# Moving three q turns of a TensorE-bound attention and MLP kernel: one behind the first x tile, one back onto TensorE, one behind the loads of batch 2

## The chip, the cores and the metric

The kernel runs on one core of one Trainium2 chip. Times are device microseconds (us) of one execution of the whole program. A profile shows a span that is about 1.8 us shorter than the measured time: the profiled execution of the kernel before measured 294.14 us and its span is 292.4 us.

Names: PE is TensorE (PEld its weight loads), ACT ScalarE, DVE VectorE, POOL GpSimd and SP SyncE. A *turn* is a transpose: it brings a [128 rows x 512] piece of q or x into the layout that a matmul needs. It is done either on PE (four 128x128 transposes through PSUM, then a copy by ACT or DVE) or by a DMA that transposes on its way ("DMA_TRANSPOSE", issued by SP).

## The reference

```python
def _attn_ref(q, k, v, g_norm):              # q, k, v: [8 batches, 8 heads, 576, 64] f32
    kv = np.einsum('bhsd,bhse->bhde', k, v)  # no softmax: one 64x64 matrix per head
    out = np.einsum('bhsd,bhde->bhse', q, kv)
    rms = np.sqrt(np.mean(out * out, axis=-1, keepdims=True) + 1e-06)
    return out / rms * g_norm

def _moe_ref(x, g_ln, w_ch1, w_ch2):         # x: [8, 576, 512], w_ch1: [512, 2048], w_ch2: [2048, 512]
    mu = np.mean(x, axis=-1, keepdims=True)
    var = np.mean((x - mu) ** 2, axis=-1, keepdims=True)
    xn = (x - mu) / np.sqrt(var + 1e-06) * g_ln
    return x + np.maximum(xn @ w_ch1, 0.0) @ w_ch2
```

The attention output of a batch, its heads side by side, is the x of the MLP. The matmuls take bf16; loads by GpSimd's queue cast on the way.

## The kernel before

The 8 x 576 rows are cut into 36 *tiles* of 128 rows, nine for each pair of batches. A batch gives four whole tiles (*slots* 0 to 3) and 64 rows that are left. The leftovers of two batches share one tile, so each batch has a *fifth slot* with 64 rows of its own and 64 of zeros. For batches 0 and 1 that shared tile is tile 8; batch 2 starts with tile 9.

The program is not written in the order in which it runs. It lists steps, each with an engine, a cost, a sorting key and what it depends on. A small planner in Python simulates the engines and sorts the steps, and they are issued in that order. Moving one step can therefore move others, on any engine.

The q of batch 0 is loaded slot by slot; slots 0 to 3 turn on PE and the fifth by DMA:

```python
for t in (1, 2, 3):
    add_q_turn_pe(0, t, load["q", 0, t], (-4.5, pos[2] - 9, pos[3] - 9)[t - 1],
                  ("ACT", "ACT", "DVE")[t - 1])
...
add_q_turn_dma(0, 4, 5, load["q", 0, 4] + [z1[0]], pos[8] - 41)
adone[0]["qfree"] = adone[0]["qT", 4][0]
```

The q of batch 1 arrives as one load (`qb`). ACT permutes it slot by slot into `qp`; slots 0 and 1 turn on PE, slots 2 and 3 in one DMA, and the fifth in another DMA behind it:

```python
if t < 2:
    add_q_turn_pe(1, t, [qperm, z1[1]], key + 1, ("DVE", "ACT")[t % 2])
elif t > 2:
    add_q_turn_dma(1, *((2, 4) if t == 3 else (4, 5)), [qperm, z1[1]], key + 1)
```

Batch 2's fifth slot of q is loaded into the buffer of batch 0's, so that load waits for batch 0's fifth-slot turn (`qfree`). When all of batch 2's q has landed, ACT permutes it in two pieces, and one DMA turns all five slots; PE then multiplies tile 9's outputs.

GpSimd issues the loads in a fixed order:

```python
pool_load(("q", 0, 1), load_slot(qp[0], q, 0, 1), rate1)
load_w(0, 1)                                   # w_ch1 in four quarters of 512 columns
pool_load(("q", 0, 2), load_slot(qp[0], q, 0, 2), rate1)
load_w(1, 1)
pool_load(("q", 0, 3), load_slot(qp[0], q, 0, 3), rate1)
load_w(2, 1)
load_w(3, 1)
... # zeroing of buffers, then load_w_kv1:
load_w(0, 2)
pool_load(("k", 1), load_kv(kb, k, 1), rate6)
pool_load(("v", 1), load_kv(vb, v, 1), rate6)
load_w(1, 2)
pool_load(("q", 1), load_q(1, 0, 4), rate4, [])
load_w(2, 2)
load_w(3, 2)
```

The first eight tiles run in small pieces (128 rows at a time); from tile 8 on, PE runs *blocks* of 512 rows. The first block matmul, at about 84 us, is used below as a milestone.

Of the kernel before, what the change touches and what calls it, by code (L numbers as in the profile page):

```python
# [14 lines left out]
def kernel(  # L15
# [35 lines left out]
    BANKS = {"mm": 4, "out": 2, "kvt": 2}  # L51
    WARM_FROM = 1.3
    HALVED = (0,)
    SPLIT_STORE = (25,)
    HALF_TURN = (0, 1)
    PARTS = ((0, 4), (4, 8))

# [39 lines left out]
    def add(eng, occ, dur, key, deps, fn, dma=None, alloc=None, main=False, lag=0.0):  # L97
        s = Step()
        s.eng, s.occ, s.dur, s.key, s.fn = eng, occ, dur, key, fn
        s.deps = [d for d in deps if d is not None]  # L100
        s.dma, s.alloc, s.main, s.frees, s.behind = dma, alloc, main, None, None
        s.start = s.done = None
        s.lag = lag
        steps.append(s)
        return s
# [85 lines left out]

    def add_dma(eng, key, deps, fn, nbytes, rate, occ=None, lat=None, tail=None):
        if eng == "POOL":
            s = add(eng, occ or 0.67, 0, key, deps, fn, dma=(1.0, nbytes / rate / 1e3, 0.6))
        else:
            s = add(eng, occ or 0.55, 0, key, deps, fn,
                    dma=(0.6 if lat is None else lat, nbytes / rate / 1e3,
                         0.75 if tail is None else tail))
        return s
# [85 lines left out]
    pos, okey = {}, {}  # L285
    last_pos = {}
    for i, (k_, n, c) in enumerate(groups):
        if k_ == "m1f":
            pos.setdefault(n, i)
            okey.setdefault(n, pos[n] - 20)  # L290
        elif k_ == "m1" and c == 0:
            for j in range(4):
                pos[4 * n + j] = i
                okey[4 * n + j] = i + {2: (-24, 4), 3: (-38, 6)}.get(n, (-44, 8))[0] + j * {2: 4, 3: 6}.get(n, 8)
        elif k_ == "m2":
            last_pos[n] = i

# [9 lines left out]
    load = {}  # L307
# [11 lines left out]
    for eng, f, dst in (("ACT", slice(0, Dm), "gl"), ("DVE", slice(Dm, Dm + D), "gn")):  # L319
        s = add("PE", *((1.8, 2.0) if dst == "gl" else (0.4, 0.6)), -98, row + [ones_done], lambda f=f: spread(f), alloc="mm")  # L320
# [97 lines left out]
    def add_q_turn_pe(b, t, deps, key, eng, h0=0, h1=H):  # L418
        w = (h1 - h0) / H
        s = add("PE", 0.24 * w, 0.24 * w + 0.26, key, [ident] + list(deps), lag=2.0 if t == 4 else 0.0, fn=  # L420
                lambda: q_turn_pe(b, t, h0, h1), alloc=("mm", "kvt")[b])
        occ, dur = act_cost(512 * w) if eng == "ACT" else dve_cost(512 * w, 1.92)
        e = add(eng, occ, dur, key, [s],
                lambda: q_turn_out(b, t, h0, h1, nc.scalar if eng == "ACT" else nc.vector))
        s.frees = e
        adone[b].setdefault(("qT", t), []).append(e)

    def q_turn_dma(b, t0=0, t1=5):
        if "qT" not in att[b]:
# [2 lines left out]
            att[b]["qT"][:, 4 * t0:4 * t1, :],  # L432
            qp[b % 2][:, t0:t1, :, :].rearrange("p t h d -> p (t h d)"))

    def add_q_turn_dma(b, t0, t1, deps, key):
        s = add_dma("SP", key, deps, lambda: q_turn_dma(b, t0, t1), 520.0 * (t1 - t0), 1.0,
                    occ=0.6 * (t1 - t0) + 0.1, lat=0.25, tail=0.42)
        for t in range(t0, t1):
            adone[b].setdefault(("qT", t), []).append(s)

    def kv_mm(b, hps):
        ps = psum.tile([128, HP, 128], f32, tag="kvt", name="kv_ps", bufs=BANKS["kvt"])
# [212 lines left out]
    for h0, h1 in PARTS:  # L655
        add_q_turn_pe(0, 0, load["q", 0, 0, h0], -57 + h0 / 4, ("DVE", "ACT")[h0 // 4], h0, h1)
    for t in (1, 2, 3):
        add_q_turn_pe(0, t, load["q", 0, t], (-4.5, pos[2] - 9, pos[3] - 9)[t - 1],
                      ("ACT", "ACT", "DVE")[t - 1])
    kvs = []  # L660

    urgent = []
    for i, (h0, h1) in enumerate(((0, 4), (4, 6), (6, 8))):
        hps = range(h0 // 2, h1 // 2)
        w = (h1 - h0) / 8
        s = add("PE", 1.36 * w, 1.36 * w + 0.25, -60 + i, load["v", 0, h0] + [k0p[h0 // 4]],
                lambda hps=hps, i=i: kv_mm(0, hps), alloc="kvt")
# [16 lines left out]
    load_w_kv1()  # L684
    pool_load(("q", 0, 4), load_fifth(qp[0][:, 4, :, :], q, 0), 180.0, [])
    pool_load(("q", 1, 4), load_fifth(qp[1][:, 4, :, :], q, 1), 180.0, [])
    add_q_turn_dma(0, 4, 5, load["q", 0, 4] + [z1[0]], pos[8] - 41)
    adone[0]["qfree"] = adone[0]["qT", 4][0]


# [1 line left out]
    def plan_batch(b):  # L692
# [3 lines left out]
        if b == 1:  # L696
            for h0, h1 in ((0, 4), (4, 8)):
                kperm.append(add("ACT", 1.2, 1.35, p - 18, load["k", 1],
                                 lambda h0=h0, h1=h1: k_permute(nc.scalar, 1, h0, h1)))
            for t in range(5):  # L700
                key = (p - 17 + 3 * t) if t < 4 else pos[8] - 40
                if t < 4:
                    qperm = add("ACT", *act_cost(512), key, load["q", 1],
                                lambda t=t: q_permute(nc.scalar, 1, t, t + 1))
                    qread = qperm
                else:
                    qperm = load["q", 1, 4][0]
                if t < 2:
                    add_q_turn_pe(1, t, [qperm, z1[1]], key + 1, ("DVE", "ACT")[t % 2])
                elif t > 2:  # L710
                    add_q_turn_dma(1, *((2, 4) if t == 3 else (4, 5)), [qperm, z1[1]], key + 1)
            vdeps = load["v", 1]
            adone[1]["qread"] = qread
            adone[1]["qfree"] = adone[1]["qT", 4][0]
        else:
            f = FIRST[b]
            def gate(n):

                if b >= 3:
                    m, i = divmod(n, 4)  # L720
                    pool_do(0.1, lambda: nc.gpsimd.tensor_copy(  # L721
                        mark, blk[m]["xT"][:, 0, i * 128:i * 128 + 1]), done[n]["xT"])
            def gate_turn():
                if b >= 3:
                    pool_do(0.1, lambda: nc.gpsimd.tensor_copy(
                        mark, att[b - 1]["qT"][:, 0, 0:1]), [adone[b - 1]["qfree"]])
            dk = [adone[b - 2]["kvmm"]]
            if b < 4:

                pool_do(0.5, lambda: nc.gpsimd.memset(kp[b % 2][no_fifth(b), 4, :, :], 0.0), dk)  # L730
            gate(f - 8 if b > 3 else 5)
            gate_turn()
            by_slot = b >= 3
            if by_slot:
                pool_load(("k", b), load_slots(kp[b % 2], k, b), rate1, dk)
            else:
                pool_load(("k", b), load_kv(kb, k, b), rate4, dk)
            pool_load(("k", b), load_fifth(kp[b % 2][:, 4, :, :], k, b), 180.0, dk)
            def some_q():
                gate(f - 7 if b > 3 else 6)  # L740
                if by_slot:
                    pool_load(("q", b), load_slots(qp[b % 2], q, b), rate1, [adone[b - 2]["qfree"]])
                else:
                    pool_load(("q", b), load_q(b, 0, 4), rate4, [adone[b - 1]["qread"]])
                pool_load(("q", b), load_fifth(qp[b % 2][:, 4, :, :], q, b), 180.0,
                          [adone[b - 2]["qfree"]])
            def some_v():
                gate(f - 6 if b > 3 else 7)
                pool_load(("v", b), load_kv(vb, v, b), rate4, dk)
                pool_load(("v", b), load_fifth(v5[b % 2], v, b), 100.0, dk)  # L750
            for load_some in (some_v, some_q) if b == 2 else (some_q, some_v):
                load_some()
            for h0, h1 in ((0, 4), (4, 8))[by_slot * 2:]:
                kperm.append(add("ACT", 0.85, 1.0, ok - 16, load["k", b][0:1] + dk,
                                 lambda h0=h0, h1=h1: k_permute(nc.scalar, b, h0, h1)))
            qperm = []
            for t0, t1 in ((0, 2), (2, 4))[by_slot * 2:]:
                qperm.append(add("ACT", 0.85, 1.0, ok - 14, load["q", b][0:1] + [
                    adone[b - 2]["qfree"]], lambda t0=t0, t1=t1: q_permute(nc.scalar, b, t0, t1)))
            for x in kperm + qperm:  # L760
                x.lag = 4.0 if b == 2 else 6.0
            kperm += load["k", b]
            turn = add_dma("SP", ok - 12, qperm + load["q", b] + (
                adone[b - 3].get("outs", []) if b >= 3 else []),
                           lambda: q_turn_dma(b), 2.6e3, 1.0, occ=2.98, lat=0.25, tail=0.42)
            for t in range(5):
                adone[b]["qT", t] = [turn]
            adone[b]["qfree"] = turn
            turn.lag = 5.0 if by_slot else 0.0
            adone[b]["qread"] = qperm[-1] if qperm else None  # L770
            vdeps = load["v", b]
# [12 lines left out]
    def plan_tile(n):  # L784
# [4 lines left out]
        deps = []  # L789
# [39 lines left out]
        for h0, h1 in ((0, 4), (4, 8)) if n in HALF_TURN else halves:  # L829
# [12 lines left out]
            else:  # L842
                turned.append(add_dma("SP", q0 + 9, [xc, m1_before], lambda: t_turn_dma(n),
                              0.5e3, 1.0, occ=1.235, lat=0.25, tail=0.42))
        dn["xT"] = turned
        var = [mean]
        if few:
            var.append(add("ACT", 0.68, 0.83, p + 5, xs + dn["xT"], lambda: t_s2(n)))
# [85 lines left out]
    for i, (kind, a, c) in enumerate(groups):  # L934
# [4 lines left out]
                need_tile(4 * a + j)  # L939
        plan_group(i, kind, a, c)  # L940


    def idle_mm(count):
        if "idle" not in blk[0]:
# [50 lines left out]
```

## Time and profile before

| | |
|---|---|
| measured | 294.01 us median of 3 (293.92 to 295.03) |
| span in the profile | 292.4 us |
| PE busy | 284.2 us, 97% |
| next busiest: DVE, ACT | 164.4 us, 143.4 us |
| PE idle ahead of matmuls | 4.74 us in all: 4.07 before 21 us, 0.07 at 39.06, 0.61 at 69.03 |

From the page of the kernel before: busy time, share of the span and instructions of each engine; then the granted clock in 40 slices of the span (9 is full).

```profile
PE 284.2 (97%) x2049; PEld 161.3 (55%) x2049; DVE 164.4 (56%) x357; ACT 143.4 (49%) x292; POOL 65.9 (23%) x93
...
PEclk9999999999999999999999999999999999999999
```

PE is the bottleneck, at full clock. A change of this kind can win only what PE idles, and must pay for all that it adds to PE. The idle time is found in PE's timeline: start in us, duration, line, operation, tile, shape, count, and in brackets the idle time before the group and what ended it. Four stretches of it, before:

```profile
15.55 0.29 PE L550 MATMUL xT_ps<-identity,xc 128*128 128x128 bf16 x2 [0.64 <-DVE xc L543]
16.18 0.40 PE L410 MATMUL qT_ps<-identity,qp 128*128 128x128 bf16 x4 [0.34 <-DMA qp<-in_q_dram]
16.41 0.28 PE L550 MATMUL xT_ps<-identity,xc 128*128 128x128 bf16 x2
...
17.15 0.94 PE L600 MATMUL mm_ps<-xT,w 128*128 128x128 bf16 x14 [0.35 <-ACT xT L557]
17.93 0.39 PE L469 MATMUL out_ps<-kv_pack,qT 128*128 128x128 bf16 x4
18.99 1.07 PE L600 MATMUL mm_ps<-xT,w 128*128 128x128 bf16 x16 [0.68 <-DMA w<-in_moe_w_ch_dram]
...
39.06 0.40 PE L410 MATMUL qT_ps<-identity,qp 128*128 128x128 bf16 x4
...
68.04 0.39 PE L550 MATMUL xT_ps<-identity,xc 128*128 128x128 bf16 x4
69.03 0.62 PE L469 MATMUL out_ps<-kv_pack,qT 128*128 128x128 bf16 x8 [0.61 <-DMA qT<-qp]
```

At 16.18 PE stands 0.34 us for the load of q slot 2, between the two halves of the turn of tile 0's x (L550). Then it stands 0.35 us at 17.15 because x came late, and 0.68 us at 18.99 for the second quarter of w_ch1. At 69.03 it stands 0.61 us for batch 2's q turn. The chain of waits (start, duration, what), followed back from the end, passes through the loads and that turn:

```profile
19.23 19.13 DMA qb<-in_q_dram
...
38.38 0.63 ACT qp L390
...
39.06 0.40 PE qT_ps L410 x4
...
62.45 6.54 DMA qT<-qp
...
69.03 0.62 PE out_ps L469 x8
```

Read it from below: the outputs at 69.03 waited for a turn issued at 62.45; and the PE turn at 39.06 (batch 1, slot 0) waited for ACT, which waited for batch 1's q to land at 38.36. The step at 39.06 shows 0.07 us of idle time.

The DMA turns in SP's queue (the issue of each, with SP's own time for it):

```profile
40.59 5.96 SPq L431 DMA_TRANSPOSE qT<-qp  x3
48.71 3.15 SPq L647 DMA_DIRECT2D out_dram<-x  x4
62.45 3.12 SPq L431 DMA_TRANSPOSE qT<-qp  x1
```

The three turns from 40.59 on are slots 2 and 3 of batch 1, then batch 0's fifth slot (issued at 43.92, landed at 51.78) and last batch 1's fifth slot (issued at 45.31, landed at 53.62). Among the waits (engine, tile, line, released by: us in total, times, longest) is GpSimd's for batch 0's fifth slot, before it may issue batch 2's fifth-slot load:

```profile
POOL qp L256 <- DMA qT<-qp: 10.0, 1, 10.0
```

### The profile page before, as it was taken

To read this page: it belongs to the slowest core of one execution; us is meant where nothing else is said; L and a number is where in the kernel's file an instruction comes from. 1 tells how busy PE (TensorE), PEld (TensorE's weight loads), DVE (VectorE), ACT (ScalarE), POOL (GpSimd) and SP (SyncE) were. 2 spreads that over 40 slices of the span, in tenths; PEclk is the share of its full clock that TensorE was granted. 3 is DMA by queue.
4 is the path that set the end of the run, shared out by engine and by line. 5 is a ranking of instruction groups with operands and counts; after the bars stand their busy time and mean duration, and the time that the engine had idled before them with its cause. 6 is when DMAs were issued, how large, how long until landed. Compare 5 with 4: busy or idle time off the path is not lost.

```text
span 292.4 us, 5167 instructions
## 1 busy us (share of the span) xinstructions
PE 284.2 (97%) x2049; PEld 161.3 (55%) x2049; DVE 164.4 (56%) x357; ACT 143.4 (49%) x292; POOL 65.9 (23%) x93
## 2 busy tenths in 40 slices
PE   8869999999999999999999999999999999999995
PEld 6759945976745445444544445444544444444444
DVE  1597048468883997557655775477557755320022
ACT  3469954887846612761276127611761177017400
POOL 8983320105506405404050406000000000000000
PEclk9999999999999999999999999999999999999999
DMA  7999999943998997993999399932101310120012
GB/s 96 186 199 205 204 198 178 252 73 70 173 171 136 158 183 161 174 203 77 188 103 161 98 181 119 168 81 91 56 18 54 92 54 18 57 86 22 0 74 72
DMA packets 109116, 35.73 MB, mean 122 GB/s; under 512 B 87715, under 2 KB 104739, under 8 KB 109092
## 3 DMA queue, kind: packets, MB, share of 16 engines
q0 software_dynamic: 72624, 18.35, 64.8%
q1 hardware_dynamic: 36228, 16.92, 25.2%
q8 instruction: 16, 0.26, 0.4%
q10 hardware_dynamic: 240, 0.13, 0.2%
q14 instruction: 8, 0.07, 0.1%
HBM read 36.70 MB, written 9.44 MB: 158 GB/s over the span
## 4 chain that ended last, share of the span: by engine, by line
PE 83%; DMA 9%; POOL 6%; issue 0%; ACT 0%; DVE 0%; POOLq 0%
PE mm_ps L634 41%; PE mm_ps L615 33%; DMA qb<-in_q_dram 7%; PE mm_ps L600 4%; PE out_ps L469 3%; PE kv_ps L446 2%; DMA qT<-qp 2%; POOL qp L262 1%; POOL w L342 1%; POOL vb L241 1%; POOL kb L241 1%; PE xT_ps L550 1%; POOL w L344 0%; ACT qp L390 0%; PE qT_ps L410 0%
## 5 line engine op out<-in xcount | busy, mean ns | idle before, releaser
L634 PE MATMUL mm_ps<-w,m 128*128 128x512 bf16 (+2 forms) x608 | 129.5, 368 | 0.0
L615 PE MATMUL mm_ps<-xT,w 128*128 128x512 bf16 x448 | 100.6, 379 | 0.0
L622 ACT ACTIVATE m<-mm_ps 128x512 bf16<-128x512 f32 x112 | 66.8, 597 | 50.3 <-PE mm_ps L615 49.4
L634 PEld LDWEIGHTS <-m 128*128 128x128 bf16 x608 | 57.2, 98 | 60.8
L615 PEld LDWEIGHTS <-w 128*128 128x128 bf16 x448 | 43.1, 98 | 48.8
L491 DVE TENSOR_REDUCE ss<-sq 128x8 f32<-128x512 f32 (+1 forms) x37 | 24.8, 669 | 49.3 <-ACT sq L482 49.3
L641 DVE SCALAR_TENSOR_TENSOR x<-mm_ps,rstd,x 128x512 f32<-128x512 f32 (+2 forms) x38 | 27.3, 720 | 41.8 <-PE mm_ps L634 41.7
L482 ACT ACTIVATE sq<-out_ps 128x512 f32<-128x512 f32 (+1 forms) x37 | 21.6, 583 | 38.4 <-PE out_ps L469 38.3
L600 PE MATMUL mm_ps<-xT,w 128*128 128x128 bf16 x512 | 31.0, 219 | 1.2 <-DMA w<-in_moe_w_ch_dram 0.7
L600 PEld LDWEIGHTS <-w 128*128 128x128 bf16 x512 | 29.3, 98 | 2.5 <-issue 0.9
L543 DVE SCALAR_TENSOR_TENSOR xc<-x,mv,gl 128x512 bf16<-128x512 f32 (+1 forms) x38 | 27.2, 724 | 1.2
L486 DVE TENSOR_TENSOR xg<-out_ps,gn 128x512 f32<-128x512 f32 (+1 forms) x37 | 24.7, 668 | 0.2
L607 ACT ACTIVATE m<-mm_ps 128x512 bf16<-128x512 f32 x32 | 18.5, 597 | 3.2 <-PE mm_ps L600 2.9
L721 POOL COPY mark<-xT 128x1 bf16<-128x1 bf16 x15 | 6.3, 422 | 54.5 <-DMA xT<-xc 52.1
L495 ACT ACTIVATE rms<-ss,eps_attn 128x8 f32<-128x8 f32 (+1 forms) x37 | 11.1, 299 | 12.3 <-DVE ss L491 12.2
L521 DVE TENSOR_TENSOR x<-xg,inv 128x512 f32<-128x512 f32 x24 | 16.6, 691 | 0.8
L537 DVE BATCH_NORM_STATS2 stats<-x 128x6 f32<-128x512 f32 x24 | 16.6, 690 | 0.5
L469 PE MATMUL out_ps<-kv_pack,qT 128*128 128x128 bf16 x160 | 14.5, 219 | 1.3 <-ACT qT L390 0.7
L469 PEld LDWEIGHTS <-qT 128*128 128x128 bf16 x160 | 11.3, 98 | 8.1 <-ACT qT L390 1.1
L446 PEld LDWEIGHTS <-kp 128*128 128x128 bf16 (+1 forms) x168 | 10.6, 101 | 1.9 <-issue 0.3
L446 PE MATMUL kv_ps<-vb,kp 128*128 128x128 bf16 (+1 forms) x144 | 11.3, 226 | 0.2
L557 ACT COPY xT<-xT_ps 128x512 bf16<-128x512 bf16 (+1 forms) x14 | 7.3, 522 | 8.1 <-PE xT_ps L550 8.1
(63 smaller groups left out, 175.2 us busy)
## 6 DMA issues: line engine op xcount, KB each, us to landing
out_dram<-x SPq DMA_DIRECT2D x31, 256.0 KB, 2.3
w<-in_moe_w_ch_dram POOLq DMA_DIRECT2D x8, 512.0 KB, 12.0
vb<-in_v_dram POOLq DMA_DIRECT2D x6, 512.0 KB, 10.9
kp<-in_k_dram POOLq DMA_DIRECT2D x5, 512.0 KB, 8.5
qp<-in_q_dram POOLq DMA_DIRECT2D x5, 512.0 KB, 9.6
qb<-in_q_dram POOLq DMA_DIRECT2D x2, 512.0 KB, 19.1
out_dram<-x SPq DMA_DIRECT2D x8, 128.0 KB, 2.7
qp<-in_q_dram POOLq DMA_DIRECT2D x10, 64.0 KB, 8.7
```

The source lines that it names most:

```text
L446: nc.tensor.matmul(ps[:, hp, :], lhsT=kp[b % 2][p, t, 2 * hp:2 * hp + 2, :].rearrange("p h d -> p (h d)"), rhs=(v5[b % 2][:, 2 * hp:2 * hp ...
L469: nc.tensor.matmul(o3[:, hp, :], lhsT=att[b]["qT"][:, 4 * t + hp, :], rhs=kv_pack[b % 3][:, hp, :], start=(i == 0), stop=(i == len(bs) - 1))
L482: nc.scalar.activation(sq[:, h0:h1, :], st[n]["ps", h0][:, h0:h1, :], func=AF.Square)
L486: nc.vector.tensor_mul(xg[:, h0:h1, :], st[n]["ps", h0][:, h0:h1, :], gn.to_broadcast([128, h1 - h0, D]))
L491: nc.vector.tensor_reduce(ss[:, h0:h1, :], st[n]["sq"][:, h0:h1, :], axis=AX.X, op=ALU.add)
L543: nc.vector.scalar_tensor_tensor(xc[:, f0:f1], in0=st[n]["x"][:, f0:f1], scalar=blk[m]["mv"][:, i, 0:1], in1=gl[:, f0:f1], op0=ALU.subtrac ...
L600: nc.tensor.matmul(ps[:, d, :], lhsT=w1[c][:, kk, d * 128:(d + 1) * 128], rhs=blk[m]["xT"][:, kk, i * 128:(i + 1) * 128], start=(kk == 0), ...
L607: nc.scalar.activation(st[n]["m1"][:, c, :, :], st[n]["m1ps", c], func=AF.Relu)
L615: nc.tensor.matmul(ps, lhsT=w1[c][:, kk, d * 128:(d + 1) * 128], rhs=blk[m]["xT"][:, kk, :], start=(kk == 0), stop=(kk == nKm - 1))
L622: nc.scalar.activation(blk[m]["m1", c][:, d, :], blk[m]["m1ps", g], func=AF.Relu)
L634: nc.tensor.matmul(st[n]["m2ps", f0], lhsT=m1_piece(n, c, d), rhs=w2[c][:, d, f0:f1], start=(c == 0 and d == 0), stop=(c == 3 and d == 3))
L641: nc.vector.scalar_tensor_tensor(x[:, f0:f1], in0=st[n]["m2ps", f0], scalar=blk[m]["rstd"][:, i, :], in1=x[:, f0:f1], op0=ALU.mult, op1=AL ...
```

## The change

It has two parts. **Part A** puts the turn of q slot 2 of batch 0 behind both half turns of tile 0's x, so that x no longer waits for the load of slot 2 at 16.18. **Part B** takes the turn of batch 0's fifth slot back from DMA to PE, and moves the DMA turn of batch 1's fifth slot from about 45 us to about 53 us, behind the loads of batch 2. The aim is to let those loads land earlier and to remove the 0.61 us wait at 69 us. Two smaller edits (a second store split in two near the end; a planner constant that yields three more warm-up matmuls) come along.

```diff
-    SPLIT_STORE = (25,)
+    SPLIT_STORE = (23, 25)
@@ planner's model of a GpSimd load
-            s = add(eng, occ or 0.67, 0, key, deps, fn, dma=(1.0, nbytes / rate / 1e3, 0.6))
+            s = add(eng, occ or 0.67, 0, key, deps, fn, dma=(1.0, nbytes / rate / 1e3, 0.9))
@@ part A
-        add_q_turn_pe(0, t, load["q", 0, t], (-4.5, pos[2] - 9, pos[3] - 9)[t - 1],
-                      ("ACT", "ACT", "DVE")[t - 1])
+        q_turned = add_q_turn_pe(0, t, load["q", 0, t], (-4.5, pos[1] - 3.7, pos[3] - 9)[t - 1],
+                                 ("ACT", "ACT", "DVE")[t - 1])
+        if t == 2:
+            behind_first = q_turned
...
+        if n in HALVED:                      # tile 0; tp is its last half turn
+            behind_first.deps.append(tp)
@@ part B
-    add_q_turn_dma(0, 4, 5, load["q", 0, 4] + [z1[0]], pos[8] - 41)
+    add_q_turn_pe(0, 4, load["q", 0, 4] + [z1[0]], pos[8] - 50, "DVE")
...
-                    add_q_turn_dma(1, *((2, 4) if t == 3 else (4, 5)), [qperm, z1[1]], key + 1)
+                    add_q_turn_dma(1, *((2, 4) if t == 3 else (4, 5)), [qperm, z1[1]],
+                                   key + 1 if t == 3 else pos[8] - 29)
...
+    for s in late_turns:                     # DMA turns of a fifth slot
+        s.deps.append(mains_made[pos[8] - 31])
```

(Cut: `add_q_turn_pe` returns its step, `late_turns` is filled in `add_q_turn_dma`, and a line is rewritten without effect. This and the later cuts are shortened.)

## The prediction

> **What bounds the kernel now.** TensorE. The page gives PE 284.2 us busy of a span of 292.4 (97%) at full granted clock. Summing the idle gaps ahead of matmuls in the timeline gives about 4.7 us: some 4.0 us before 21 us, 0.07 us at 39.06, and 0.61 us at 69.03, where the first output matmuls of batch 2 wait for its q turn ("DMA qT<-qp" in the chain of waits, 6.54 us from 62.45). After 69 us PE never waits. So the change can win only those gaps; what it adds to PE after 21 us is paid in full.
>
> **Part A, slot 2's turn behind both turns of tile 0's x.** In the timeline PE stands at 16.18 for the load of q slot 2 (0.34 us idle), so the second half of x turns at 16.41 and the first-layer matmuls wait until 17.15 (0.35 us). Turning x first brings those about 0.5 us forward. But the next 16 need the second weight quarter, which lands at 18.95 (0.68 us idle before 18.99, "DMA w"). The load order is unchanged, so that wait should grow by what part A saves. After it PE's order is unchanged to about 49 us. I expect zero from part A. Three extra warm-up matmuls shift the first kv matmul by under 0.1 us; that wait absorbs it.
>
> **Part B, the fifth slots.** From 40.6 to 54 us three DMA turns (slots 2 and 3 of batch 1, then the two fifth slots; landing 49.3, 51.8, 53.6) share the 16 DMA engines with the loads of batch 2. The Trainium skill ("Trainium Kernel Development and Optimization", Key Constraints) says that queues run on the same 16 engines and interleave; the packets agree: the load queue alone moves about 400 KB per 2 us, at 46 to 48 us only 157 KB beside 159 KB of turns. GpSimd also waits 10.0 us ("POOL qp <- DMA qT<-qp") for batch 0's turn before it can issue the next fifth-slot load, at 52.34. Batch 2's q lands at 60.41, ScalarE permutes it for 2 us, its turn is issued at 62.45 and releases PE at 69.03.
> After: one slot's turn (128 KB, about 1 us of DMA time at the rate just read, an estimate) leaves the DMAs, and batch 1's moves to about 53 us, behind four stores. Batch 2's q should land 0.6 to 1 us earlier, and its turn should finish near 68.2. PE reaches that point at about 68.25, so the 0.61 us wait should nearly vanish. Cost: four 128x128 transposes, 0.22 us of PE, and one 0.42 us VectorE copy off the path. Net about -0.4 us, less some 0.1 us for what remains of the wait or for a new one.
>
> **Predicted**: 293.7 us, 80% range 293.2 to 294.4. Faster by over 2%: 0.005; within 2%: 0.985; slower by over 2%: 0.01.
>
> **What would show it.** A: idle before the matmuls at about 19 us grows to about 1.1 us, and what follows starts at 19.0 as before. B: batch 2's q lands before 60; its turn is issued near 61.6; the wait at 69 is under 0.2 us; PE has four more turn matmuls near 49.7. From 70 us on every stage is shifted by the same amount.
>
> **What would make it wrong.** Batch 1's late turn, behind the stores, may land after 60.6, when PE wants tile 8's outputs: a new wait of up to 1 us would turn the gain into a loss. Batch 2's q may not land earlier, and then PE pays 0.22 us for nothing. The second weight quarter may land at another time. The new order of evictions may stall PE on PSUM.

## The result, and the profile after

| | before | after |
|---|---|---|
| measured, median | 293.97 us (6 runs, 293.81 to 295.03) | 294.20 us (6 runs, 293.93 to 294.74) |
| ratio | | 1.0006, 95% interval 0.9988 to 1.0023 |
| span in the profile | 292.4 us | 292.3 us |
| PE's last matmul ends (trace) | 288.92 us | 288.82 us |

A ratio is the mean time of one kernel's fast runs over that of the other's of the same rounds, so it is not quite the ratio of the medians. The kernel after is the same within 2%, and inside the predicted range; but of the predicted gain of 0.3 us nothing is to be seen here, although the profile shows almost everything that was predicted. PE's timeline after, in the same stretches:

```profile
15.56 0.68 PE L556 MATMUL xT_ps<-identity,xc 128*128 128x128 bf16 x4 [0.65 <-DVE xc L549]
16.08 0.39 PE L411 MATMUL qT_ps<-identity,qp 128*128 128x128 bf16 x4
16.31 1.34 PE L606 MATMUL mm_ps<-xT,w 128*128 128x128 bf16 x16
17.48 0.39 PE L475 MATMUL out_ps<-kv_pack,qT 128*128 128x128 bf16 x4
19.13 1.07 PE L606 MATMUL mm_ps<-xT,w 128*128 128x128 bf16 x16 [1.26 <-DMA w<-in_moe_w_ch_dram]
...
39.52 0.40 PE L411 MATMUL qT_ps<-identity,qp 128*128 128x128 bf16 x4 [0.39 <-ACT qp L391]
...
50.14 0.39 PE L411 MATMUL qT_ps<-identity,qp 128*128 128x128 bf16 x4
...
68.72 0.61 PE L475 MATMUL out_ps<-kv_pack,qT 128*128 128x128 bf16 x8
69.17 0.39 PE L556 MATMUL xT_ps<-identity,xc 128*128 128x128 bf16 x4
```

Part A did what it should and won nothing: x turns in one piece, the outputs of L475 start 0.45 us earlier (17.48, before 17.93), and the wait for the second weight quarter grew from 0.68 to 1.26 us. Part B too: four more transposes at 50.14, and at 68.72 no wait at all. But the step at 39 is a *gate*, which PE cannot pass before the load of batch 1's q has landed: it now shows 0.39 us of idle time, and comes 0.46 us later (39.52, before 39.06). The chain says why:

```profile
9.59 9.50 DMA w<-in_moe_w_ch_dram
...
19.37 19.45 DMA qb<-in_q_dram
...
38.84 0.63 ACT qp L391
...
39.52 0.40 PE qT_ps L411 x4
...
68.88 0.45 PE out_ps L475 x8
```

The DMA turn of batch 2 has left the chain. The load of batch 1's q is still in it, and it landed at 38.82 instead of 38.36. Ahead of it stands the load of the second weight quarter, and this is no accident of one trace: GpSimd issues batch 1's q only after that quarter has landed (the two loads use the same semaphore). In all ten profiles in which neither of the two loads was moved, the issue comes 0.28 us after the quarter's landing. The gates at 19 and 39 us are thus links of one chain. Of the 0.46 us, 0.14 are inherited from the quarter, and 0.32 arose while q itself was loading (19.45 us, before 19.13). SP's queue and GpSimd's waits, after:

```profile
41.04 1.33 SPq L433 DMA_TRANSPOSE qT<-qp  x1
49.17 3.50 SPq L653 DMA_DIRECT2D out_dram<-x  x4
52.78 11.89 SPq L433 DMA_TRANSPOSE qT<-qp  x2
```

```profile
POOL qp L256 <- PE qT_ps L411: 8.1, 1, 8.1
POOL qb L248 <- DMA w<-in_moe_w_ch_dram: 0.4, 1, 0.4
```

One turn at 41, four stores, and the late turn at 52.78, grouped with batch 2's (issued at 61.74, before 62.45). GpSimd waits 8.1 us instead of 10.0, now for the turn on PE. The second line is the wait of batch 1's q for the weight quarter.

The four whole slots of batch 2's q landed 1.66 us earlier (58.75, before 60.41), but its turn was issued only 0.71 us earlier. ACT's timeline of the two permutes in between, before and then after, tells why:

```profile
60.43 1.99 ACT L390 COPY qp<-qb 128x1024 bf16<-128x1024 bf16 x2 [0.60 <-DMA qb<-in_q_dram]
```

```profile
59.73 1.98 ACT L391 COPY qp<-qb 128x1024 bf16<-128x1024 bf16 x2
```

Before, ACT waited for the load. After, it was busy with earlier work for 0.98 us past the landing. The turn landed at 68.26 us instead of 68.98; PE wanted it 0.46 us later, at 68.72.

Nothing that PE waits for differs later. The stretch from 84 to 289 us in both kernels (length, then busy us and instructions of PE, PEld, DVE, ACT and POOL, clock, share of the DMA engines, GB/s), before and then after:

```profile
84.00:289.00 205.00, 204.92 (x1133) 100.73 (x1130) 113.18 (x215) 86.76 (x165) 30.98 (x39) 1.00 0.77 105
```

```profile
84.00:289.00 205.00, 204.82 (x1132) 100.74 (x1130) 112.27 (x213) 86.74 (x165) 30.52 (x39) 1.00 0.80 103
```

In the records of all 14 profiles, the time from the first block matmul to the end of PE's last is 205.02 us. From there to the end of the span it is 3.45 us in the kernel before and 3.46 after, so the split store shows no worth. So everything is decided before 84 us, and that milestone alone need be followed.

For these two executions the sum can be written down. The second weight quarter landed 0.14 us later (19.09, before 18.95). The gap at the gate grew by 0.32 us (0.067 to 0.387), the extra loading time of q. The four transposes took 0.22 us. The wait at 69 that went was worth 0.77 us, not the 0.61 shown: before, the x turn started at 68.04 and the outputs behind it at 69.03, which is 0.99 us, and four transposes in a row take 0.22 us of that (they start 0.22 us before what follows them, as at 69.17 to 69.39 after). The sum 0.14 + 0.32 + 0.22 - 0.77 is -0.09 us; PE's end moved by -0.10. The Trainium skill ("Perfetto Trace Analysis", Summary: the profiler window per engine type) says that a TensorE record reaches to an *estimated* end; this trace agrees, with 0.39 us shown for transposes that hold PE for 0.22, and idle time read up to a modelled end is 0.16 us short.

### The profile page after: what moved, and what is told of

Read it like the earlier page. It is cut to its first block, busy times and chain, and to the rows that moved or that the text cites. A ratio compares the mean times of both kernels' runs of the same rounds, so it can differ in the third digit from the quotient of the medians.

```text
span 292.3 us, 5180 instructions
## 1 busy us (share of the span) xinstructions
PE 283.5 (97%) x2056; PEld 160.9 (55%) x2056; DVE 164.3 (56%) x358; ACT 143.2 (49%) x292; POOL 65.7 (22%) x93
## 3 DMA queue, kind: packets, MB, share of 16 engines
q0 software_dynamic: 72624, 18.35, 66.6%
## 4 chain that ended last, share of the span: by engine, by line
PE 85%; DMA 10%; POOL 3%; issue 0%; ACT 0%; DVE 0%; POOLq 0%
PE mm_ps L640 41%; PE mm_ps L621 33%; DMA qb<-in_q_dram 7%; PE mm_ps L606 5%; DMA w<-in_moe_w_ch_dram 3%; PE out_ps L475 3%; PE kv_ps L452 2%; POOL qp L262 1%; POOL vb L241 1%; PE xT_ps L556 1%; POOL kb L241 1%; PE qT_ps L411 0%; POOL w L343 0%; ACT qp L391 0%; POOL identity masks.py:197 0%
## 5 line engine op out<-in xcount | busy, mean ns | idle before, releaser
L730 POOL COPY mark<-xT 128x1 bf16<-128x1 bf16 x15 | 7.0, 464 | 58.0 <-DMA xT<-xc 54.0
L475 PEld LDWEIGHTS <-qT 128*128 128x128 bf16 x160 | 11.4, 98 | 7.2 <-ACT qT L391 1.1
L475 PE MATMUL out_ps<-kv_pack,qT 128*128 128x128 bf16 x160 | 14.5, 219 | 0.7 <-ACT qT L391 0.7
L467 DVE CAST kv_pack<-kv_ps 64x256 bf16<-64x256 f32 (+2 forms) x17 | 6.6, 390 | 9.8 <-PE kv_ps L452 5.9
L269 POOL DMA_DIRECT2D qp<-in_q_dram x5 | 11.4, 2282 | 0.7 <-issue 0.7
```

Of the source, the lines that this page charges most:

```text
L475: nc.tensor.matmul(o3[:, hp, :], lhsT=att[b]["qT"][:, 4 * t + hp, :], rhs=kv_pack[b % 3][:, hp, :], start=(i == 0), stop=(i == len(bs) - 1))
```

## The experiments

Two theories stood against each other.

- **Theory 1: scatter.** Landings of loads differ between executions of the same kernel by as much as the effect. The two late landings were chance, and part B is worth its few tenths once they are averaged out.
- **Theory 2: given back.** The change itself delays the second weight quarter or batch 1's q (through part A's new order at 16 us or otherwise), and so gives back at 39 us what it wins at 69.

A third question is which half of part B works, and a fourth whether a different order could move the gates at 19 and 39 us. Kernels of one job share a chip and the runs of the kernel before.

### Both kernels again, and each part alone

`before_again` and `after_again` are unchanged copies. `a_only` is the kernel before with part A and the planner constant. `b_only` is the kernel after without part A:

```diff
 a_only, against the kernel before
+ dma=(1.0, nbytes / rate / 1e3, 0.9)
+ slot 2's key pos[1] - 3.7;  if n in HALVED: behind_first.deps.append(tp)
 b_only, against the kernel after
- slot 2's key pos[1] - 3.7
+ slot 2's key pos[2] - 9
- if n in HALVED: behind_first.deps.append(tp)
```

> The kernel before once more, unchanged, for a second profile. Theory 1 (scatter of the loads): the landing of the second weight quarter (18.95 us in the first profile of before, 19.09 after) and of batch 1's q (38.36 before, 38.82 after) differ from execution to execution by some tenths of a us whatever the kernel, so this profile shows values that differ from 18.95 and 38.36 by 0.1 to 0.5 us, and a wait of TensorE ahead of batch 1's first q turn (about 39 us) between 0 and 0.5 us. The wait at 69 us is there again, 0.3 to 0.7 us. Theory 2 (the change delays these loads): 18.95 and 38.36 come back within 0.1 us. Time ratio 1.000 either way, which also shows what the timing resolves.

> The changed kernel once more, unchanged. Theory 1: the wait ahead of batch 1's first q turn is again anywhere from 0 to 0.5 us, not tied to 0.39; the wait at 69 us is gone again; ratio to before 0.998 to 1.000. Theory 2: the late landings come back, 19.09 and 38.82 within 0.1 us, and the wait of 0.39 us with them; ratio 1.000 to 1.001.

> Part A alone: q turn of slot 2 behind both turns of tile 0's x, fifth slots as before. Theory 1: worth zero, since the matmuls that come forward run into the wait for the second weight quarter, which grows from 0.68 to about 1.2 us; the wait at 69 us is back at 0.5 to 0.8 us; ratio 0.999 to 1.001. Theory 2 (part A delays the loads by some tenths): landings near 19.1 and 38.8, ratio 1.001 to 1.002.

> Part B alone: fifth slots as in the changed kernel, slot 2's turn between the two turns of tile 0's x as before; the order of every engine differs from the changed kernel in nothing else. Theory 1: as the changed kernel, within 0.1 per cent; the wait at 69 us gone, 0.22 us of added turns, so about 0.5 us less from 60 to 70 us than before. Wait for the second weight quarter near 0.7 us, not 1.26. Theory 2 with part A as the culprit: landings near 18.95 and 38.4 and a ratio of 0.998, clearly below the changed kernel's.

The kernel before had a median of 294.38 us over 11 runs on that chip.

| | median us | ratio to before | 95% interval |
|---|---|---|---|
| before_again | 294.41 | 0.9997 | 0.9985 to 1.0009 |
| after_again | 293.86 | 0.9985 | 0.9972 to 0.9998 |
| a_only | 294.49 | 1.0007 | 0.9995 to 1.0019 |
| b_only | 294.15 | 0.9990 | 0.9978 to 1.0003 |

The same change that gave 1.0006 in its first six runs gave 0.9985 here. Part A alone gains nothing. In its profile the wait ahead of the second quarter is 0.96 us (about 1.2 was expected), and the wait at 69 is still there (0.35 us, where 0.5 to 0.8 was expected). Its order on PE differs from the kernel before also in a few places from 52 us on, where the planner placed turns anew; at 69 us the outputs now stand ahead of the x turn. PE's timeline of a_only:

```profile
19.50 1.01 PE L601 MATMUL mm_ps<-xT,w 128*128 128x128 bf16 x15 [0.96 <-DMA w<-in_moe_w_ch_dram]
...
68.96 0.62 PE L470 MATMUL out_ps<-kv_pack,qT 128*128 128x128 bf16 x8 [0.35 <-DMA qT<-qp]
```

And of before_again, where the wait at 69 is half of what the first profile of the same kernel showed:

```profile
68.81 0.62 PE L469 MATMUL out_ps<-kv_pack,qT 128*128 128x128 bf16 x8 [0.30 <-DMA qT<-qp]
```

In b_only that wait is gone:

```profile
68.10 0.61 PE L475 MATMUL out_ps<-kv_pack,qT 128*128 128x128 bf16 x8
```

The first column of that line is the lesson: the outputs start at 68.10 here and at 68.72 in the kernel after, with the same order of work from 21 us on. The difference was there at 39 us. ACT's permutes of batch 1's q start when it has landed. ACT's timeline, before, after and b_only:

```profile
38.38 2.18 ACT L390 COPY qp<-qb 128x512 bf16<-128x512 bf16 x4 [2.27 <-DMA qb<-in_q_dram]
```

```profile
38.84 2.17 ACT L391 COPY qp<-qb 128x512 bf16<-128x512 bf16 x4 [2.60 <-DMA qb<-in_q_dram]
```

```profile
38.23 2.18 ACT L391 COPY qp<-qb 128x512 bf16<-128x512 bf16 x4 [2.24 <-DMA qb<-in_q_dram]
```

Three executions, three landings; in all the profiles in which this turn was neither moved nor its load swapped, the PE turn starts 0.69 to 0.70 us after the landing (0.63 us of permute, then 0.05 to 0.07).

Theory 2 makes a claim that the table below can refute. All 14 profiles, in us from the span's start, read from the trace's records; "stretch" is the time from the first q turn of batch 1 on PE to the first block matmul, in which part B works (the rows from early_turn on come from the experiments that follow):

| profile | second quarter lands | batch 1's q lands | batch 2's q lands | wait at 69 | stretch | PE ends |
|---|---|---|---|---|---|---|
| before | 18.95 | 38.36 | 60.41 | 0.61 | 44.84 | 288.92 |
| before_again | 18.97 | 38.45 | 60.16 | 0.30 | 44.53 | 288.69 |
| a_only | 19.45 | 38.77 | 60.36 | 0.35 | 44.59 | 289.07 |
| after | 19.09 | 38.82 | 58.75 | 0 | 44.28 | 288.82 |
| after_again | 19.15 | 38.63 | 58.25 | 0 | 44.28 | 288.63 |
| b_only | 18.82 | 38.20 | 57.69 | 0 | 44.28 | 288.20 |
| early_turn | 19.36 | 38.67 | 58.88 | 0 | 44.28 | 288.68 |
| dma_fifth | 19.14 | 38.40 | 60.57 | 0.49 | 45.12 | 289.23 |
| late_q1 | 18.98 | 39.34 | 58.97 | 0 | 43.92 | 288.98 |
| late_q1_two | 19.93 | 39.41 | 58.88 | 0 | 42.65 | 289.22 |
| early_w | 18.35 | 38.98 | 57.44 | 0 | 42.65 | 289.70 |
| swap_b | 19.05 | 35.81 | 60.91 | 0.20 | 47.00 | 289.23 |
| swap_after | 18.94 | 35.73 | 60.34 | 0 | 46.55 | 288.65 |
| swap_before | 19.68 | 36.25 | 61.77 | 0 | 46.58 | 289.43 |

From late_q1 down the first q turn is itself moved, so those stretches are not compared with the others. In swap_after and swap_before PE waits 0.15 and 0.32 us at about 69 us for x, not for q.

The second quarter landed at 19.09, 19.15, 19.45 and 18.94 us in the four kernels with part A in its own form (mean 19.16), and between 18.82 and 19.93 in the nine without it (mean 19.21; early_w, whose loads are reordered, is left out). Part A does not delay it in any way that shows. In all 14 the first matmul of that quarter starts 0.04 to 0.05 us after its landing, so the time at which earlier matmuls are ready does not matter: that is why part A is worth nothing. Batch 1's q landed between 38.63 and 38.82 us in the three kernels with part A and its load order unchanged (mean 38.74), and between 38.20 and 39.41 in the seven without part A (mean 38.69), although five of these seven lie at or below 38.67. Part of that difference is the quarter's, since q is issued 0.28 us after it. From its own issue to its landing, q took 19.04 to 19.45 us with part A (mean 19.23) and 18.97 to 20.07 without it (mean 19.24, or 19.10 without the 20.07 of late_q1).

The two copies alone do not decide it. before_again came out as theory 2 had said: 18.97 and 38.45, both within 0.1 us of the first profile. after_again went against theory 2: 19.15 came back within 0.1 us, but q landed 0.19 us earlier than in the first profile of after, and the wait at the gate was 0.12 us, not 0.39.

The measured times point the same way: with part A 0.9985 (after_again), without it 0.9990 (b_only). And one kernel scatters by itself: b_only's six runs on one chip took 293.44 to 294.44 us, all at a clock of 1.0, although its last 205 us are the same in every profile. Over all profiles theory 2 finds little support, and scatter is enough to explain the first result. A delay of batch 1's q of 0.3 us (0.1%) by part A is about what these intervals could still hide, so it is not excluded. What makes one execution's load late was not isolated, but the traces show one source. In the two profiles with the latest second quarter, late_q1_two (19.93) and swap_before (19.68), GpSimd issued that load at 10.36 and 10.09 us, after waiting 0.83 and 0.45 us for the landing of an earlier k load; in the others with this load order it was issued at 9.51 to 9.75.

The stretch column takes the scatter upstream out. It is 44.84, 44.53 and 44.59 without part B, and 44.28 in all three profiles with it. Part B is worth 0.25 to 0.56 us there, depending on how late batch 2's q turn would have been, with its 0.22 us of transposes already paid.

### Which half of part B works

`early_turn` has only batch 0's turn back on PE; batch 1's DMA turn keeps its old place. `dma_fifth` has only the late DMA turn; batch 0's stays on DMA.

```diff
 early_turn, against b_only
-                                   key + 1 if t == 3 else pos[8] - 29)
+                                   key + 1)
-    for s in late_turns:
-        s.deps.append(mains_made[pos[8] - 31])
 dma_fifth, against b_only
-    add_q_turn_pe(0, 4, load["q", 0, 4] + [z1[0]], pos[8] - 50, "DVE")
+    add_q_turn_dma(0, 4, 5, load["q", 0, 4] + [z1[0]], pos[8] - 41)
-    for s in late_turns:
+    for s in late_turns[1:]:
```

> Part B without the move: batch 0's fifth slot on TensorE, but batch 1's DMA turn back at its old place, straight behind the first turn (part A left out, as in b_only). Theory 1a (what helps is that one turn leaves the DMA queues, not that the other moves): batch 2's q lands as in b_only (57.7 to 58.8 us), no wait at 69, and from batch 1's first q turn to the first block matmul 44.3 us as in b_only, against 44.5 to 44.8 before. Theory 1b (the move behind the loads is what helps): batch 2's q lands at 59.5 us or later, its turn is issued near 62 and the wait at 69 is back at 0.2 us or more. Either way the ratio to before lies between 0.998 and 1.001.

> Part B without the return to TensorE: batch 0's fifth slot turned by DMA again at its old place, batch 1's late as in the changed kernel (part A left out). Theory 1a: the same DMA work as before is in the way of batch 2's q, so it lands near 60 us, GpSimd waits near 10 us for batch 0's turn, TensorE waits 0.1 to 0.6 us near 68.5 and does not pay the 0.22 us of turns: 44.3 to 44.6 us from batch 1's first q turn to the first block matmul. Theory 1b: batch 2's q lands before 59 us and the wait is gone: 44.1 us. Ratio to before 0.998 to 1.001.

Measured on another chip, with the kernel before at 294.16 us: early_turn 293.95 us, ratio 0.9991 (0.9979 to 1.0004); dma_fifth 294.71 us, ratio 1.0018 (1.0006 to 1.003). In early_turn's profile the stretch is 44.28 us, as expected, and nothing waits at 69. In dma_fifth's it is 45.12, where 44.3 to 44.6 was expected, and the ratio lies above the range that was expected too: PE waits twice. Its timeline on PE:

```profile
60.81 0.56 PE L475 MATMUL out_ps<-kv_pack,qT 128*128 128x128 bf16 x7 [0.22 <-DMA qT<-qp]
...
69.12 0.62 PE L475 MATMUL out_ps<-kv_pack,qT 128*128 128x128 bf16 x8 [0.49 <-DMA qT<-qp]
```

So the half that works is batch 0's fifth slot on PE: with it, and with the loads in their old order, batch 2's q lands at 57.7 to 59.0 us, without it at 60.2 to 60.6. The later DMA turn wins nothing that shows. Alone it loses, because the late turn lands after PE wants tile 8's outputs (0.22 us at 60.81). That is the risk which the prediction named; in the kernel after it was missed by 1.2 us (turn landed at 59.80, outputs wanted at 61.02).

Why the load lands earlier is only half told. Two things change together: a slot's worth of turning leaves the DMA engines, and batch 2's fifth-slot load is issued earlier, at 50.8 instead of 52.34 us, since it waits for PE's turn rather than the DMA's. No run separates them, and the two are not enough in every load order: swap_b and swap_after below have both (the fifth-slot load is issued at 50.35 and 50.22), and q still lands at 60.91 and 60.34. That loads and turns share the engines is what the Trainium skill says ("DMA: Bandwidth & Descriptors", Issuing engines are not separate DMA queues), and the packets before agree: the load queue moves about 400 KB in 2 us alone (40 to 42 us), and 157 KB beside 159 KB of turns (46 to 48 us). The two stretches are not quite alike: the loads' packets were about 810 bytes on average in the first and 250 in the second. At 42 to 44 us, with packets of 260 bytes and no turn, the load queue moved 356 KB, which is the fairer number to compare with.

### Can the gate at 39 us be moved?

`late_q1` and `late_q1_two` hold both PE turns of batch 1 back behind the 20th and the 21st group of main matmuls, so that PE has work while the load comes in. `early_w` is the kernel after with the second weight quarter loaded ahead of q slot 2, and with the turns held back as in late_q1_two.

```diff
 late_q1, against b_only (late_q1_two: mains_made[20])
+    for s in q1_turns:                       # the steps of add_q_turn_pe(1, t, ...)
+        s.deps.append(mains_made[19])
 early_w, against the kernel after
-    pool_load(("q", 0, 2), load_slot(qp[0], q, 0, 2), rate1)
     load_w(1, 1)
+    pool_load(("q", 0, 2), load_slot(qp[0], q, 0, 2), rate1)
+    slot 3's turn behind tile 1's last turn;  q1_turns behind mains_made[20]
```

> b_only with the first q turns of batch 1 placed one second-layer group (four matmuls, 0.86 us) later on TensorE. Theory 1: what sets the time at 39 us is the landing of batch 1's q (38.2 to 38.8) plus 0.6 us of ScalarE; with one group more ahead of it TensorE has something to do and the small wait there (0.04 to 0.39 us in five profiles) is gone in every profile, worth 0 to 0.4 us; the rest of the program is shifted by the same amount; ratio to before 0.997 to 0.9995. Theory 2: no wait there is caused by scatter, so nothing is won: 0.999.

> Part B alone, batch 1's first q turns two second-layer groups later on TensorE than in b_only, loads as before. Theory 1: TensorE gets to the turn at 40.6 us or later, after any landing seen so far (38.2 to 39.3, plus 0.7), so no wait; 64.2 to 64.35 us between the same two matmuls; ratio to before 0.997 to 0.9995 and as swap_b within 0.001. Rival: tile 4's x comes too late for its turn near 48 us and a new wait appears there or at the first-layer matmuls after it.

> A candidate: the changed kernel with the second weight quarter loaded ahead of q slot 2, slot 3's q turn behind both turns of tile 1's x, and batch 1's q turns two groups later. Theory 1: the wait near 19 us is for that quarter alone, so loading it one slot earlier (q slot 2 took 0.8 us of landing) brings it to about 18.2 us and the program forward by up to 0.7 us; since batch 1's q turns stand later, the landing near 38.5 does not take it back; ratio to before 0.995 to 0.999. Rival: the loads as a whole bind the first 40 us, or slot 2 is missed instead, new waits appear near 20 and 22 us, and the ratio is 0.999 to 1.002.

| | median us | ratio to before | 95% interval |
|---|---|---|---|
| late_q1 (beside early_turn) | 294.23 | 1.0000 | 0.9986 to 1.0013 |
| early_w (beside early_turn) | 294.95 | 1.0033 | 1.0021 to 1.0045 |
| late_q1_two (third chip; before 294.22) | 293.72 | 0.9983 | 0.9968 to 0.9997 |

late_q1 did not get past the gate: in its profile batch 1's q landed at 39.34 us, later than in any profile so far, and even the delayed turn (at 40.03) waited for it. ACT's timeline of late_q1:

```profile
39.36 2.18 ACT L391 COPY qp<-qb 128x512 bf16<-128x512 bf16 x4 [3.21 <-DMA qb<-in_q_dram]
```

One group later the turn no longer waits. PE's timeline of late_q1_two:

```profile
41.55 0.61 PE L411 MATMUL qT_ps<-identity,qp 128*128 128x128 bf16 x8
```

Its q landed even later (39.41), and PE did not idle there. From the second quarter's first matmul to the first block matmul it took 64.22 us, as expected, where the profiles of the kernel after took 64.67 and 64.41. The profiled execution was still its slowest run (294.44 us); in it the second weight quarter landed at 19.93, the latest of all. The ratio of 0.9983 is the lowest, but its interval contains after_again's 0.9985, so it is not shown to be better than the change.

early_w shows a limit. Its weight quarter landed at 18.35 us, 0.6 us earlier than in the kernel before and earlier than in any other profile, and still the kernel was slower by 0.3%, where a gain of 0.1 to 0.5% was expected. In the profile PE then ran at half clock for one window. Busy time and clock by windows of early_w (columns as above), the stretch ahead of it and the half-clock stretch:

```profile
15.15:18.57 3.42, 1.96 (x23) 1.38 (x24) 3.32 (x9) 2.15 (x6) 3.09 (x5) 1.00 1.80 181
18.57:21.98 3.41, 3.32 (x33) 2.97 (x31) 1.18 (x5) 1.20 (x4) 2.41 (x3) 0.50 1.27 205
```

The Trainium skill ("TensorE: Matmul & The Clock Gate", Part 1: The HAM clock gate) has PE fall to half clock after an idle window of about 3.4 us. The length agrees (3.41 us at 0.50). But PE was not idle in the stretch ahead of it: there were 23 matmuls, and their records cover 1.96 of 3.42 us. In after_again a stretch of the same length with as much covered time kept its clock:

```profile
16.61:20.02 3.41, 1.93 (x33) 1.75 (x33) 3.31 (x9) 2.22 (x6) 3.08 (x5) 1.00 1.53 193
```

The covered time is the wrong measure, since each record reaches to a modelled end. The counts in brackets differ: 33 matmuls here, 23 in early_w. In the clock records, changes are whole steps of 3.41 us apart (early_w's three stretches last 10.24, 3.41 and 273.07 us). Of all stretches that lie on these steps between 8 and 24 us in the 14 profiles, early_w's has the fewest matmuls; the next have 28 and were followed by full clock. So the half clock came after the emptiest stretch. It is one case, a trace can miss a few matmuls, and no run tested where the limit lies.

But the half clock is not the whole cause. Three of early_w's five runs had a mean clock of 1.0 and took no less (294.88, 295.5 and 294.87 us). What slows early_w in those runs is open.

### An earlier load of batch 1's q

The last idea was to load batch 1's q one place earlier, ahead of the second quarter of w_ch2, in b_only, after and before.

```diff
 swap_b, swap_after, swap_before: in load_w_kv1 of b_only, after and before
-        load_w(1, 2)
         pool_load(("q", 1), load_q(1, 0, 4), rate4, [])
+        load_w(1, 2)
```

> Part B alone, with batch 1's q loaded ahead of the second quarter of the second-layer weights instead of behind it. Theory 1 (in every profile so far TensorE's first q turn of batch 1 starts 0.69 to 0.70 us after that load lands, so its landing dates all that follows): q lands near 35.7 us, about 2.7 us earlier, the turn starts when TensorE gets to it, near 37.2, without a wait; from the first matmul of the second weight quarter (about 19.0) to the first block matmul (about 83.2) 64.2 to 64.35 us, the lowest value seen so far (64.25 to 64.91), whatever the loads do; the time follows the 19 us wait alone. Ratio to before 0.997 to 0.999. Rival: the swapped weight quarter, landing near 38.4, makes a new wait near 38 to 40 us, and nothing is won.

> The changed kernel (A and B) with the same swap of two loads. Theory 1, part A worth zero even with the wait at 39 us out of the way: 64.2 to 64.35 us from the first matmul of the second weight quarter to the first block matmul, wait ahead of that matmul 0.3 to 0.5 us longer than in swap_b's profile at the same landing; ratio within 0.001 of swap_b's. Rival (part A is worth its 0.3 to 0.5 us, hidden by the wait at 39): 0.001 to 0.002 below swap_b.

> The kernel before with the same swap of two loads, so without A and B. Theory 1: B's worth in the stretch from 40 to 84 us is paid out without the scatter at 39: the wait near 69 is back at 0.3 to 0.8 us, 64.5 to 65.0 us from the first matmul of the second weight quarter to the first block matmul, ratio 0.001 to 0.002 above swap_b and swap_after. If part B were worth nothing, the three would lie within 0.0005.

Measured beside late_q1_two: swap_b 294.87 us, ratio 1.0019 (0.9996 to 1.0041); swap_after 294.01 us, 0.9994 (0.9978 to 1.0011); swap_before 294.69 us, 1.0010 (0.9991 to 1.003). Batch 1's q landed 2 us or more earlier (35.73 to 36.25 us) and nothing was won. From the second quarter's first matmul to the first block matmul swap_b and swap_after took 65.11 and 64.65 us, where 64.2 to 64.35 was expected; swap_before took 64.68, inside the 64.5 to 65.0 expected of it. But swap_before did not come out behind both others, as theory 1 wanted: its ratio lies between theirs, its time between the two matmuls is 0.03 us from swap_after's, and PE shows no wait for batch 2's q in it, where 0.3 to 0.8 us was expected. So part B's gain is shown for the old load order only. Once that q lands earlier, its DMA turn is issued earlier too. SP's queue in swap_b and in b_only:

```profile
38.12 1.33 SPq L433 DMA_TRANSPOSE qT<-qp  x1
```

```profile
40.43 1.32 SPq L433 DMA_TRANSPOSE qT<-qp  x1
```

At 38 us the turn runs beside loads that are still coming in. Batch 2's k, behind them, lands at 49.95 instead of 47.96 us, its q at 60.91 instead of 57.69, and in swap_b the wait that part B had removed is back (0.20 us at 68.83):

```profile
68.83 0.62 PE L475 MATMUL out_ps<-kv_pack,qT 128*128 128x128 bf16 x8 [0.20 <-DMA qT<-qp]
```

The order of the two is shown; that the turn's overlap causes the later landing is the likely reading, not a separate test. swap_after against swap_b (0.9994 and 1.0019, overlapping intervals) says nothing about part A that the table does not.

## Why the prediction was right and where it was not

- **Bound by TensorE, only the gaps can be won: right.** From the first block matmul on, every profile takes 205.02 us.
- **Part A is worth zero: right**, for the reason given. The wait for the second weight quarter took it all: predicted about 1.1 us, measured 1.26 in the first profile and 0.96 alone in a_only. The 0.34 us stall at 16.18 was itself not steady: in before_again the PE gaps around 16 us are 0.06 and 0.12 us.
- **Batch 2's q lands before 60, its turn is issued near 61.6, the wait at 69 is under 0.2 us: right.** It landed at 58.75, the turn was issued at 61.74, and the wait was gone. But the figures behind it met by luck. "0.6 to 1 us earlier" was too small: it was 1.7 us in the first pair. The estimate counted only the DMA time of one slot's turn; whether the earlier issue of the fifth-slot load makes the rest is not shown. And the prediction let ACT permute at once, while ACT was busy for 0.98 us more. The two errors cancelled, and the turn landed at 68.26 us, where 68.2 was predicted.
- **The turn of PE costs 0.22 us and the net is about -0.4 us: right for the stretch, but the terms differ.** The removed wait was worth 0.77 us in that execution, not 0.61, because idle time up to a modelled end understates it. The wait also differs by execution (0.61, 0.30, 0.35), so the predicted 0.4 us lies within the 0.25 to 0.56 us that the stretches show.
- **"What follows starts at 19.0 as before", and a shift that is the same from 70 us on with a net of -0.4: this step failed in the first comparison.** The prediction took all up to 40 us as fixed. The second quarter landed 0.14 us later, which passed on to batch 1's q, and q took 0.32 us longer to load; this ate the gain in the profiled execution. The runs do not show that the change adds to these landings, and they show scatter that is large enough: they range over 1.1 and 1.2 us in kernels with the same load order. The prediction did list the landing of the weight quarter as a risk, but not batch 1's q at 39.06, although the chain of waits before shows it as a 19.13 us piece that ends there.
- **The time.** 293.7 us was predicted, 0.999 of the time before. The change measured 1.0006, then 0.9985; b_only and early_turn measured 0.9990 and 0.9991, and late_q1 and late_q1_two, which hold part B too, 1.0000 and 0.9983. The mean of the six is about 0.999, which is what was predicted; but only the intervals of after_again and late_q1_two exclude 1, so the gain is likely rather than proved. That the first comparison lies inside the range says little, since its change points the other way. The evidence for the gain is the stretch in the profiles more than the measured times.

## What to carry to other kernels

When a load's landing releases PE, work brought forward ahead of that point is worth nothing, and the scatter of the landing dates all that follows. Compare executions from the last such gate on, not from the start of the span, before you credit or blame a change of a few tenths of a microsecond. A short gap in front of a step that a load releases is a gate all the same: look at when the step starts relative to the landing, not at how long the engine idled. And ask what a late load delays in the queue: here a late weight quarter at 19 us meant a late issue, and so a late landing, of the q at 39 us.

A turn on a full TensorE can be the cheaper one: for 0.22 us of PE, a load that PE was waiting for later landed over 1 us earlier, and in the first pair 0.7 us of that reached the turn behind it. Loading something earlier also moves what it triggers; here the earlier q released its DMA turn into the stretch where the loads were densest.

## What the Trainium skill lacked or had wrong

- "Perfetto Trace Analysis" says that TensorE ends are estimated, but not by how much a wait is then misread: a wait shown as 0.61 us held PE for 0.77 us start to start, behind 128x128 transposes shown as 0.39 us that hold PE for 0.22.
- "TensorE: Matmul & The Clock Gate" gives an idle window as the condition for the half clock, but not how little work counts as idle. Here 3.41 us at half clock followed 3.42 us with 23 matmuls, while 3.41 us with 33 matmuls in another run kept the full clock, though the records covered as much of it (1.93 and 1.96 us).
- "DMA: Bandwidth & Descriptors" says that queues interleave, with no figure for what a DMA turn costs the loads beside it. Here the load queue moved 157 KB in 2 us beside 159 KB of turns, 316 KB in all. With packets of about the same size and no turn it moved 356 KB, so the sum fell a little too.
- "Runtime: NRT & Kernel Launch", Instruction fetch mechanics, calls the refill of instructions in 16 KiB blocks mostly hidden. Each of the 14 traces shows one such packet, of 0.89 to 0.98 us, started between 15.76 and 17.52 us, while the second weight quarter was coming in. In after_again 15 of that quarter's 16 shares had landed by 17.95 us and the last at 19.15. Whether the packet delays that share is not known: no run tested it.
- No page says how far the landing of a load scatters between executions: over kernels with the same order of loads, 1.1 us for the second weight quarter (18.82 to 19.93) and 1.2 us for batch 1's q (38.20 to 39.41).
